# Mish and the attention copies ahead of the weight decodings in slots 4 to 15 of a three-stage kernel

## The chip, the cores and the metric

One core of a Trainium2 chip runs the whole program in one launch. The metric is device time in microseconds (us), the median of several runs. The matrix engine is called PE, the vector engine DVE, the scalar engine ACT, GpSimd POOL, and SP issues most of the DMAs.

## The reference

Three stages follow each other. Attention without softmax (4 batches, 8 heads, 576 tokens, 64 per head) gives 2304 tokens of 512 values; two feed-forward stages follow, each 512 to 2048 to 512, the first with Mish, the second with a leaky ReLU whose slope is learned.

```python
kv  = einsum('bhsd,bhse->bhde', k, v)
out = einsum('bhsd,bhde->bhse', q, kv)
x   = out / sqrt(mean(out*out, -1) + 1e-6) * g_norm      # then 2304 x 512
h   = x @ w_in1;  g = h * tanh(softplus(h));  x = g @ w_out1
h   = x @ w_in2;  g = max(h,0) + alpha*min(h,0);  out = g @ w_out2
```

The weights come as 64-bit floats and are read as pairs of 32-bit words.

## The kernel before, in words

A product of fp32 matrices is made of three fp32r products of a high and a low half (`three`, lines 135 to 137): high by high, high by low, low by high. So every operand has to be split first, on ACT (the cast that makes the high half) and DVE (the subtraction that makes the low half).

The first feed-forward stage goes over five blocks of tokens (512, 256, 512, 512, 512). A block has 16 slots, one for each 128 columns of the hidden layer; slots are numbered through. In slot s PE makes

- `mm1(s)`, 12 matmuls, the hidden values h of slot s;
- pieces of the attention of the next block (the hooks): `t_pe` transposes q (L257), `kv_pe` makes k times v (L232), `o_pe` multiplies q by it (L289);
- `mm2(s - 4)`, 12 matmuls, which adds the part of slot s - 4 to four output accumulators.

Between `mm1` and `mm2` lie `mish(s)` on ACT (L547, from h to the tile n) and `g_split(s)` (the cast to gh on ACT, L540, and the subtraction to gl on DVE, L541). `mish(s - 1)` stands in slot s (`front`), `g_split(s - 2)` at the end of slot s (`back`). Two buffers each limit this: `mish(s)` writes the n that `g_split(s - 2)` has read, and `mm1(s)` writes the bank of h that `mish(s - 2)` has read (`bank("h", ...)`, two banks).

In slots 4 to 15, the first block, the weights of this stage are decoded on the way, about two tiles of 128x512 words in each slot (three in slot 7): `w_begin` scales the high words on ACT (`w_scale`, L432), joins the words by three operations on DVE (`w_bits`, L438, L439, L442), and then finishes the tile that was begun before it: its cast on ACT (`w_high`, L477) and its subtraction on DVE (`w_low`, L481). L438 reads the low words; L439 reads the scaled high words, so it waits for L432. The decoding of a tile of `w_in1` stands in the list `mid` of a slot, that of a tile of `w_out1` in `last`.

The attention of the next block is spread over `hook`, two entries in a slot (2s and 2s + 1). After `kv_pe` come two small copies from PSUM (`kv_ev`, L244, on ACT), which `o_pe` needs; after `o_pe` a square and a copy (L296, L297). In slot 10 the hook `rsqrt_ev` part 0 loads another activation table, computes two functions (L341, L342, L345), and loads Mish's table again (L346).

From slot 4 to slot 25 the order of all engines is the order in which the code is written (`manual_schedule`); from slot 26 on only PE's is, and a scheduler orders the rest. Each engine works through its own list strictly from the front: an instruction that waits holds up all behind it on that engine.

Of the kernel before, what the change touches and what calls it, by code (L numbers as in the profile page):

```python
# [33 lines left out]
EARLY = 4  # L34
# [23 lines left out]
def attn_moe_moe2(  # L58
# [37 lines left out]
    NJ = DFF // P  # L96
# [36 lines left out]
    def three(ps, lhs, rhs, start, stop, **kw):  # L133
        (lh, ll), (rh, rl) = lhs, rhs
        nc.tensor.matmul(ps, lh, rh, start=start, stop=False, **kw)  # L135
        nc.tensor.matmul(ps, lh, rl, start=False, stop=False, **kw)  # L136
        nc.tensor.matmul(ps, ll, rh, start=False, stop=stop, **kw)  # L137
# [74 lines left out]
    def bank(tag, nm):  # L212
        if tag == "at":
            turn[0] += 1
            tag = f"at{turn[0] % 2}"
        pool = ps_h if tag == "h" else ps_a if tag[:2] == "at" else ps_acc
        return pool.tile([P, 512], F32, tag=tag, name=nm)
# [287 lines left out]
    def at_slot(kk):  # L505
        i = kk // NJ
        return i, kk % NJ, BLOCKS[i]

    def mm1(kk, chunks=range(4)):
        i, j, T = at_slot(kk)  # L510
        if chunks[0] == 0:
            hps[kk] = bank({2: "at1", 3: "acc3"}.get(kk, "h"), "h")
        ps = hps[kk]
        wh, wl = w1[0, j]
        for c in chunks:
            cs = slice(c * P, (c + 1) * P)
            three(ps[:, :T], (wh[:, cs], wl[:, cs]), (xh[i, c], xl[i, c]), c == 0, c == NP - 1)

    def mm2(kk):
        i, j, T = at_slot(kk)  # L520
        gh, gl = gt.pop(kk)
        wh, wl = w2[0, j]
        if j == 0:
            acc[i] = [None] * NP
        for m in range(NP):
            ms = slice(m * P, (m + 1) * P)
            if j == 0:
                acc[i][m] = bank(f"acc{m}", "acc")
            three(acc[i][m][:, :T], (wh[:, ms], wl[:, ms]), (gh, gl), j == 0, j == NJ - 1)
        if j == NJ - 1:  # L530
            evac(i)
# [4 lines left out]
    def g_split(kk):  # L536
        T = at_slot(kk)[2]
        g = gs.pop(kk)
        gh, gl = m_tile("gh", T, F32R), m_tile("gl", T, F32R)
        nc.scalar.copy(out=gh, in_=g)  # L540
        nc.vector.tensor_tensor(out=gl, in0=g, in1=f32(gh), op=ALU.subtract)  # L541
        gt[kk] = gh, gl

    def mish(kk):
        T = at_slot(kk)[2]
        g = m_tile("n", T)
        nc.scalar.activation(out=g, in_=hps.pop(kk)[:, :T], func=AF.Mish)  # L547
        gs[kk] = g
# [3 lines left out]
    def evac(i):  # L552
        a = acc.pop(i)
        T = BLOCKS[i]
        if not x2d:
            x2d.append(dp.tile([P, NP, NT], F32, name="x2d"))
        for c in range(0, NP, 2):
            xs = stage("xs", F32, 2 * T)
            nc.scalar.copy(out=xs[:, :T], in_=a[c][:, :T])
            nc.vector.tensor_copy(out=xs[:, T:], in_=a[c + 1][:, :T])  # L560
            nc.sync.dma_start(
                out=x2d[0][:, c : c + 2, starts[i] : starts[i] + T], in_=xs.rearrange("p (c t) -> p c t", c=2)
            )
# [363 lines left out]
    loads, early, after, late, hook, mid, fin, last = ({} for _ in range(8))  # L927
# [4 lines left out]
    def run(d, s):  # L932
        for f, a in d.pop(s, []):
            f(*a)
# [71 lines left out]
    def front(s):  # L1006
        if EARLY < s <= NS:
            mish(s - 1)

    def back(s):  # L1010
        if LAG <= s < NS + LAG:
            mm2(s - LAG)
        if s - 2 < NS:
            g_split(s - 2)

    def slot(s):
        for d in (early, loads) if s == EARLY else (loads, early):
            run(d, s)
        mm1(s)

        run(mid, s)
        run(hook, 2 * s)
        run(after, s)
        run(late, s)
        front(s)
        run(last, s)
        run(fin, s)
        back(s)
        run(hook, 2 * s + 1)
# [6 lines left out]
    def quarter(n):  # L1036

        s = NS + n
        u, step = divmod(n, 4)
        run(early, s)  # L1040
        run(late, s)

        def before(step):
            front(s)
            run(mid, s)
            back(s)
            if step == 3 or u:
                chunk(u if step == 3 else u - 1, LATER[step])

        if long(u):  # L1050
            long_unit(u, step)
            if step == 1:
                before(0)
                before(1)
            elif step == 3:
                before(2)
                prelu1(u, "12", tmp["x"], tmp["x"])
                before(3)
        elif u < NPASS * NU:
            unit(u, step, lambda: before(step))  # L1060
        else:
            before(step)
        run(fin, s)
        run(last, s)
# [32 lines left out]
    with tc.manual_schedule():  # L1097
# [36 lines left out]
        for s in range(EARLY, MANUAL):  # L1134
            slot(s)
    with tc.manual_schedule(engines={mybir.EngineType.PE}):
        for s in range(MANUAL, NS):
            slot(s)
        for n in range(4 * NPASS * NU + 3):
            quarter(n)  # L1140
# [30 lines left out]
```

## Time and profile before

| what | value |
|---|---|
| median of 3 runs | 837.09 us (836.38 to 839.85) |
| the profiled execution: its own time | 837.51 us |
| the profiled execution: its span | 835.7 us |
| granted TensorE clock, mean | 0.999 of full speed |
| ACT busy | 318.9 us (38%) |
| POOL busy | 42.9 us (5%) |
| matmuls | 4446 |

Times of the trace are counted from the start of the span. The page's busy share tells how long an engine had something in work. A matmul overlaps the next, so its duration is longer than the step to the next one; whether PE was held up is read from the steps between starts and from the idle time. The first block's slots 4 to 15 lie between about 36 and 112 us.

### The profile page before, as it was taken

Reading aid. Unit: us, or ns where it says so; the run is one execution under the profiler, and the core shown is the slowest. Engines: PE = TensorE matmul, PEld = TensorE weight load, DVE = VectorE, ACT = ScalarE, POOL = GpSimd, SP = SyncE. Lnnn points to the kernel's source line nnn. Section 1 sums busy time; section 2 is a strip of 40 time slices with the busy share of each in tenths; the row PEclk is TensorE's granted clock in tenths of the full one; section 3 lists DMA queues with packets and bytes.
Section 4 is the critical chain, followed back from the end, with each engine's and each line's share of the span. In section 5 each row is a group of like instructions: output and inputs, shape, how many; then the busy total and the mean of one; then the engine's idle time right before and its main releaser. Section 6 shows DMA issues by size and latency. Waiting matters only on the chain.

```text
span 835.7 us, 11757 instructions
## 1 busy us (share of the span) xinstructions
PE 826.6 (99%) x4446; PEld 710.4 (85%) x4446; DVE 534.5 (64%) x1001; ACT 318.9 (38%) x630; POOL 42.9 (5%) x52
## 2 busy tenths in 40 slices
PE   8999999999999999999999999999999999999998
PEld 6777789998878887888788889889999999899896
DVE  6998873552275334543978777889654668754644
ACT  5768555344433442433555322234111124211112
POOL 0000000000302121030400000000000000000000
PEclk9999999999999999999999999999999999999999
DMA  8974447244131413039995614232411332311212
GB/s 294 286 208 145 137 94 164 53 79 131 49 99 44 145 45 114 1 138 370 341 368 180 189 51 151 89 126 64 126 38 39 82 107 74 116 38 40 74 38 76
DMA packets 84377, 104.59 MB, mean 125 GB/s; under 512 B 34785, under 2 KB 57569, under 8 KB 84321
## 3 DMA queue, kind: packets, MB, share of 16 engines
q1 hardware_dynamic: 84176, 103.71, 40.0%
q8 instruction: 35, 0.57, 0.3%
q14 instruction: 22, 0.17, 0.1%
q10 hardware_dynamic: 144, 0.13, 0.0%
HBM read 79.70 MB, written 24.12 MB: 124 GB/s over the span
## 4 chain that ended last, share of the span: by engine, by line
PE 89%; DVE 5%; DMA 2%; ACT 2%; issue 0%; SPq 0%; DVEq 0%; ACTq 0%
PE acc L136 15%; PE acc L137 15%; PE acc L135 15%; PE pp L137 7%; PE pp L135 7%; PE pp L136 7%; PE h L135 7%; PE h L136 7%; PE h L137 7%; DMA ws<-in_moe_w_out_dram 1%; PE kvps L232 1%; DVE wf L439 1%; DVE wf L442 1%; DMA v<-in_v_dram 1%; PE ops L289 0%
## 5 line engine op out<-in xcount | busy, mean ns | idle before, releaser
L135 PE MATMUL acc<-gh,w 128*128 128x512 f32 (+1 forms) x320 | 119.3, 373 | 0.0
L136 PE MATMUL acc<-gl,w 128*128 128x512 f32 (+1 forms) x320 | 117.9, 368 | 0.0
L137 PE MATMUL acc<-gh,w 128*128 128x512 f32 (+1 forms) x320 | 117.9, 368 | 0.0
L541 DVE TENSOR_TENSOR gl<-n,gh 128x512 fp32r<-128x512 f32 (+1 forms) x80 | 51.7, 648 | 95.1 <-ACT gh L540 94.9
L135 PE MATMUL h<-x,w 128*128 128x512 f32 (+1 forms) x240 | 90.6, 378 | 1.2 <-ACT n L547 1.1
L137 PE MATMUL h<-x,w 128*128 128x512 f32 (+1 forms) x240 | 88.6, 369 | 0.0
L136 PE MATMUL h<-x,w 128*128 128x512 f32 (+1 forms) x240 | 88.4, 368 | 0.0
L540 ACT CAST gh<-n 128x512 fp32r<-128x512 f32 (+1 forms) x80 | 46.3, 578 | 106.8 <-PE acc L137 106.2
L137 PE MATMUL acc<-w,g 128*128 128x512 f32 x216 | 85.2, 394 | 0.0
L808 ACT CAST g<-ty 128x384 fp32r<-128x384 f32 x48 | 24.7, 514 | 138.1 <-DVE ty L806 138.0
L135 PEld LDWEIGHTS acc<-gh,w 128*128 128x128 f32 x320 | 60.3, 189 | 10.3 <-issue 0.4
L137 PEld LDWEIGHTS acc<-gh,w 128*128 128x128 f32 x320 | 60.3, 188 | 10.2
L136 PEld LDWEIGHTS acc<-gl,w 128*128 128x128 f32 x320 | 60.4, 189 | 9.8
L547 ACT ACTIVATE n<-h 128x512 f32<-128x512 f32 (+1 forms) x80 | 44.5, 556 | 34.4 <-DVE gl L541 34.3
L136 PE MATMUL acc<-w,xb 128*128 128x512 f32 x144 | 56.6, 393 | 0.0
L136 PE MATMUL acc<-w,g 128*128 128x512 f32 x144 | 56.6, 393 | 0.0
L135 PEld LDWEIGHTS h<-x,w 128*128 128x128 f32 x240 | 45.2, 188 | 13.0 <-ACT n L547 3.1
L135 PE MATMUL acc<-w,xb 128*128 128x512 f32 x144 | 56.0, 389 | 0.0
L135 PE MATMUL acc<-w,g 128*128 128x512 f32 x144 | 56.0, 389 | 0.0
L137 PEld LDWEIGHTS h<-x,w 128*128 128x128 f32 x240 | 45.2, 188 | 8.1 <-DVE w L481 0.4
L136 PEld LDWEIGHTS h<-x,w 128*128 128x128 f32 x240 | 45.3, 189 | 7.2
L137 PEld LDWEIGHTS acc<-w,g 128*128 128x128 f32 x216 | 40.5, 188 | 8.6
(230 smaller groups left out, 1706.6 us busy)
## 6 DMA issues: line engine op xcount, KB each, us to landing
xb<-wd SPq DMA_DIRECT2D x72, 256.0 KB, 2.7
ws<-in_moe_w_out_dram SPq DMA_DIRECT2D x32, 512.0 KB, 4.2
xw<-in_moe_w_in_dram SPq DMA_DIRECT2D x12, 512.0 KB, 5.6
r<-in_moe_w_in_dram SPq DMA_DIRECT2D x12, 512.0 KB, 4.2
wd<-r SPq DMA_DIRECT2D x12, 512.0 KB, 2.6
w<-wd SPq DMA_DIRECT2D x12, 512.0 KB, 6.6
k<-in_k_dram SPq DMA_DIRECT2D x16, 288.0 KB, 3.5
v<-in_v_dram SPq DMA_DIRECT2D x16, 288.0 KB, 4.5
```

Of the source, the lines that this page charges most:

```text
L135: nc.tensor.matmul(ps, lh, rh, start=start, stop=False, **kw)
L136: nc.tensor.matmul(ps, lh, rl, start=False, stop=False, **kw)
L137: nc.tensor.matmul(ps, ll, rh, start=False, stop=stop, **kw)
L232: nc.tensor.matmul(ps[hs, hs], kt[:, h, j, :], vt[:, h, j, :], start=(j == 0), stop=(j == KVJ - 1))
L439: nc.vector.scalar_tensor_tensor(out=si, in0=high, scalar=-0x80000000, in1=si, op0=ALU.bitwise_and, op1=ALU.bitwise_or)
L442: nc.vector.scalar_tensor_tensor(out=si, in0=high, scalar=3, in1=si, op0=ALU.logical_shift_left, op1=ALU.bitwise_or)
L540: nc.scalar.copy(out=gh, in_=g)
L541: nc.vector.tensor_tensor(out=gl, in0=g, in1=f32(gh), op=ALU.subtract)
L547: nc.scalar.activation(out=g, in_=hps.pop(kk)[:, :T], func=AF.Mish)
L808: nc.scalar.copy(out=h, in_=out)
```

## The change

In slot 4 the hook 9 (`kv_pe`, `kv_ev`) moves in front of `g_split(2)`, and both in front of the decoding in `last`. In slots 5 to 15 `front(s)`, which is `mish(s - 1)`, moves from behind `mid`, the even hook, `after` and `late` to a place right behind `mm1(s)`, ahead of `mid`. Nothing is added or removed.

```diff
-    def back(s):
+    def back(s, between=lambda: None):
         if LAG <= s < NS + LAG:
             mm2(s - LAG)
+        between()
         if s - 2 < NS:
             g_split(s - 2)
...
         mm1(s)
+        if s == EARLY:
+
+            run(mid, s)
+            run(hook, 2 * s)
+            back(s, lambda: run(hook, 2 * s + 1))
+            for d in (late, last, fin):
+                run(d, s)
+            return
+
+        sooner = EARLY < s < NJ
+        if sooner:
+            front(s)
 
         run(mid, s)
         run(hook, 2 * s)
         run(after, s)
         run(late, s)
-        front(s)
+        if not sooner:
+            front(s)
```

PE's list and SP's list of DMAs keep their order; ACT's list changes in slots 4 to 15, and DVE's in slot 4 alone.

On ACT in slot 4, from the copy of transposed q (L270) on, before (`keep` holds k times v, `gh` is slot 2's, w16 is a tile of `w_in1`, `ws` the raw words of the next tile):

```order
L270 COPY qT_545<-tps_542 128x256
L432 ACTIVATE ws_515<-ws_515 128x512
L477 CAST w16_552<-wf_535 128x512
L540 CAST gh_571<-n_485 128x512
L244 COPY keep_87<-kvps_575 64x64 x2
```

and with the change:

```order
L270 COPY qT_545<-tps_542 128x256
L244 COPY keep_87<-kvps_563 64x64 x2
L540 CAST gh_578<-n_485 128x512
L432 ACTIVATE ws_515<-ws_515 128x512
L477 CAST w16_587<-wf_535 128x512
```

The two copies and the cast of gh moved ahead of the scaling and the cast of the decoding.

On ACT at the border of slots 5 and 6, before (`xw` holds the raw words of the tile decoded in `mid`, n is Mish's result of slot 5):

```order
L540 CAST gh_651<-n_492 128x512
L270 COPY qT_658<-tps_655 128x256
L432 ACTIVATE xw_95<-xw_95 128x512
L477 CAST w23_681<-wf_632 128x512
L244 COPY keep_87<-kvps_684 64x64 x2
L547 ACTIVATE n_708<-h_602 128x512
L432 ACTIVATE ws_590<-ws_590 128x512
```

and with the change:

```order
L540 CAST gh_651<-n_492 128x512
L270 COPY qT_658<-tps_655 128x256
L547 ACTIVATE n_676<-h_602 128x512
L432 ACTIVATE xw_95<-xw_95 128x512
L477 CAST w23_683<-wf_632 128x512
L244 COPY keep_87<-kvps_686 64x64 x2
L432 ACTIVATE ws_590<-ws_590 128x512
```

Mish (L547) moved ahead of the scaling of the first tile of slot 6, of a cast and of the copies of k times v.

On ACT in slot 10, where the activation table is changed, before:

```order
L432 ACTIVATE xw_95<-xw_95 128x512
L477 CAST w27_975<-wf_924 128x512
L341 ACT_TABLE_LOAD
L342 ACTIVATE qT_658<-msps_978,epsb_94 128x256
L345 ACTIVATE qT_775<-qT_658 128x256
L346 ACT_TABLE_LOAD
L547 ACTIVATE n_987<-h_885 128x512
L432 ACTIVATE ws_883<-ws_883 128x512
```

and with the change:

```order
L547 ACTIVATE n_970<-h_885 128x512
L432 ACTIVATE xw_95<-xw_95 128x512
L477 CAST w27_977<-wf_924 128x512
L341 ACT_TABLE_LOAD
L342 ACTIVATE qT_658<-msps_980,epsb_94 128x256
L345 ACTIVATE qT_777<-qT_658 128x256
L346 ACT_TABLE_LOAD
L432 ACTIVATE ws_883<-ws_883 128x512
```

Mish moved from behind the second table load to the front of the slot; the second tile's scaling stays behind that load.

## Rows read from the trace of the kernel before

**Rows 1.** The page's busy times, and one stretch of the windows view (start:end us, length, busy us of PE, PEld, DVE, ACT, POOL, clock, DMA share, GB/s).

```profile
PE 826.6 (99%) x4446; PEld 710.4 (85%) x4446; DVE 534.5 (64%) x1001; ACT 318.9 (38%) x630; POOL 42.9 (5%) x52
50.00:60.00 10.00, 10.00 (x69) 8.12 (x67) 9.52 (x16) 7.45 (x17) 0.00 (x0) 1.00 0.89 242
```

**Rows 2.** Timeline of ACT, slot 4 (start us, duration us, engine, line, operation, out<-in).

```profile
43.97 0.68 ACT L432 ACTIVATE ws<-ws 128x512 f32<-128x512 f32 x1
...
46.08 0.42 ACT L244 COPY keep<-kvps 64x64 f32<-64x64 f32 x2
```

**Rows 3.** Timeline of PE, slot 5 (in brackets the idle time before, and its releaser).

```profile
41.92 0.92 PE L232 MATMUL kvps<-v,k 96*64 96x64 f32 x24
...
45.62 0.33 PE L289 MATMUL ops<-qT,keep 128*128 128x64 f32 x2
46.56 0.59 PE L289 MATMUL ops<-qT,keep 128*128 128x192 f32 x2 [0.60 <-ACT keep L244]
```

**Rows 4.** Timeline of DVE, the end of slot 5 and the beginning of slot 6.

```profile
53.76 0.68 DVE L541 TENSOR_TENSOR gl<-n,gh 128x512 fp32r<-128x512 f32 x1
54.36 0.42 DVE L438 TENSOR_SCALAR wf<-xw 128x512 int32<-128x512 int32 x1
54.89 0.69 DVE L439 SCALAR_TENSOR_TENSOR wf<-xw,wf 128x512 int32<-128x512 int32 x1
```

**Rows 5.** Timeline of ACT in slot 6: the scaling for that L439, then Mish.

```profile
52.00 0.68 ACT L432 ACTIVATE xw<-xw 128x512 f32<-128x512 f32 x1
...
54.48 0.60 ACT L547 ACTIVATE n<-h 128x512 f32<-128x512 f32 x1 [0.26 <-DVE gl L541]
54.97 0.69 ACT L432 ACTIVATE ws<-ws 128x512 f32<-128x512 f32 x1
```

**Rows 6.** Timeline of ACT in slot 10, around the two table loads.

```profile
78.49 0.62 ACT L477 CAST w<-wf 128x512 fp32r<-128x512 f32 x1
79.12 1.28 ACT L341 ACT_TABLE_LOAD   x1
80.76 0.47 ACT L342 ACTIVATE qT<-msps,epsb 128x256 f32<-128x256 f32 x1 [0.35 <-PE msps L331]
81.26 0.42 ACT L345 ACTIVATE qT<-qT 128x256 f32<-128x256 f32 x1
81.70 1.28 ACT L346 ACT_TABLE_LOAD   x1
82.99 0.60 ACT L547 ACTIVATE n<-h 128x512 f32<-128x512 f32 x1
```

**Rows 7.** Timeline of DVE: gl at the end of slots 9 to 12, and L439 waiting or first behind.

```profile
78.97 0.68 DVE L541 TENSOR_TENSOR gl<-n,gh 128x512 fp32r<-128x512 f32 x1
...
84.17 0.69 DVE L439 SCALAR_TENSOR_TENSOR wf<-ws,wf 128x512 int32<-128x512 int32 x1 [1.60 <-ACT ws L432]
...
86.11 0.68 DVE L541 TENSOR_TENSOR gl<-n,gh 128x512 fp32r<-128x512 f32 x1
...
88.03 0.69 DVE L439 SCALAR_TENSOR_TENSOR wf<-ws,wf 128x512 int32<-128x512 int32 x1
...
92.83 0.68 DVE L541 TENSOR_TENSOR gl<-n,gh 128x512 fp32r<-128x512 f32 x1
...
94.05 0.69 DVE L439 SCALAR_TENSOR_TENSOR wf<-ws,wf 128x512 int32<-128x512 int32 x1 [0.20 <-ACT ws L432]
...
98.58 0.69 DVE L541 TENSOR_TENSOR gl<-n,gh 128x512 fp32r<-128x512 f32 x1
```

**Rows 8.** Timeline of PE: the first matmul of `mm1(13)` and of `mm1(14)`.

```profile
95.08 0.50 PE L135 MATMUL h<-x,w 128*128 128x512 f32 x1 [0.24 <-ACT n L547]
...
100.96 0.40 PE L135 MATMUL h<-x,w 128*128 128x512 f32 x1
```

**Rows 9.** Timeline in slot 16: DVE's low half of w_out1's tile 12, PE's first use of it.

```profile
112.91 0.68 DVE L481 TENSOR_TENSOR w<-wf,w 128x512 fp32r<-128x512 f32 x1
...
114.17 0.39 PE L137 MATMUL acc<-gh,w 128*128 128x512 f32 x1
```

## The prediction

> **What bounds the kernel now.** I read the page's busy times first, then PE's idle times and step lengths slot by slot, and then the timelines of ACT and DVE beside them. PE is busy for 826.6 of 835.7 us [rows 1], so no reordering of the other engines can give back much; what it can do is to take away single waits of PE, or to make new ones. In the first block DVE is the engine that can make them: between 50 and 60 us it is busy for 9.52 of 10 us, and PE for all 10 [rows 1]. DVE has hardly any slack there, and ACT, busy for 7.45, has some.
>
> PE is held up visibly at two places in slots 4 to 15. In slot 5 the second part of `o_pe` starts 0.94 us after the first, 0.60 of it idle, until the copies of k times v end [rows 3]. These copies run at 46.08 although their input was ready at 42.84 (41.92 + 0.92): the scaling that started at 43.97, and more, stood ahead of them [rows 2, 3]. In slot 13 `mm1` has to wait for Mish, 0.24 us idle [rows 8]. The reader should keep both in mind as all that the change can win here: taken between idle time and lost step, 0.8 + 0.4 = 1.2 us.
>
> **What decides Mish's start.** Mish of slot s - 1 overwrites the n that gl of slot s - 3 is made from, and that gl is the last thing in DVE's list of slot s - 1. In slot 6 one sees it: gl runs from 53.76 to 54.44 [rows 4], and Mish starts at 54.48, after ACT had idled for 0.26 us waiting for just this [rows 5]. So even at its old, late place Mish waited for DVE. At its new place it waits for the same end of gl, but now with the scaling of the next tile, its cast, the copies of k times v and all else of the slot queued behind it on ACT.
>
> **Slot 4.** The copies move ahead of a scaling, a cast and the cast of gh, to where the scaling starts now, 43.97 [rows 2]. They take 0.42, so they are done 1.2 us before `o_pe` starts at 45.62 [rows 3]. PE's wait goes: 0.60 (the idle time) to 0.94 (the whole step), taken as 0.8. On DVE gl of slot 2 only changes places with the four operations of one decoding, with no work added; I cost that at nothing. The cover is that the low half of the tile needed next gets finished some 0.5 us later, one place of 0.6 down the list, still ahead of its use by PE; without that lead `mm1(6)` would wait 0.6 at most.
>
> **Slots 6 to 9, the term that matters.** DVE begins these slots with L438 and L439 of the tile in `mid`. Before, the scaling that L439 needs was done long ago (52.00 for an L439 at 54.89), and L439 started 0.45 us after gl's end (54.89 - 54.44) [rows 4, 5]. Now the order after gl's end is: 0.04 to Mish's start (54.48 - 54.44), 0.49 from Mish to the next instruction (54.97 - 54.48), 0.69 for the scaling, and for the handover to L439 another 0.04: 1.26 [rows 4, 5]. DVE therefore loses 1.26 - 0.45 = 0.81 us in every slot that begins this way with no wait before: slots 6, 7, 8 and 9, so 4 x 0.81 = 3.2 us. Slot 5 is spared, since a whole decoding stands between gl of slot 2 and the tile of slot 5's `mid`.
>
> **Slot 10, with the table loads.** Here DVE waited already: gl ended at 79.65 and the L439 of the second tile started at 84.17, 4.52 later, after 1.60 idle for ACT's scaling [rows 7]. ACT had reached the table loads at 79.12, before gl's end, because Mish stood behind them [rows 6]. Now everything follows gl's end: 0.04, Mish 0.49, scaling 0.58 (0.69 less the overlap of 0.11 that Mish shows), cast 0.63, table 1.29, 0.50, 0.44, table 1.29, scaling 0.69, handover 0.04: 5.99 us [rows 5, 6]. That is 5.99 - 4.52 = 1.5 us more. The 0.35 that ACT waited for PE [rows 6] falls away, as PE's sums are ready long before; no term of the sum holds it.
>
> For a table I use 1.29, since the rows show 1.28 for the load and the next instruction 0.01 behind the second one's end (81.70 + 1.28, then 82.99) [rows 6]. A rule of the Trainium skill speaks against the change more strongly: ScalarE: Activation LUTs, section What ACT_TABLE_LOAD costs, gives 1.28 us for the load and another 1.38 for a drain behind it. By that rule the two loads would add 2.8 us to this slot and to the sum; the second load here shows no such drain.
>
> **Slots 11 and 12.** In slot 11 two operations of the attention lie between gl (ended 86.79) and L439 (88.03): 1.24 already, so the new 1.26 costs nothing. In slot 12 L439 followed gl's end by 0.54, a late load included (94.05 - 93.51) [rows 7]; now 1.26, so 0.7 more. From slot 13 on no tile is decoded in `mid`, and the scaling behind Mish is needed later.
>
> **The sum.** DVE's delay at the end of slot 12 is 3.2 + 1.5 + 0 + 0.7 = 5.4 us: gl that ended at 99.27 [rows 7] ends at 104.67. On the way PE waits again and again, for copies of k times v that now stand behind Mish, and for Mish itself; those waits are not added, for the last one on the same chain contains them, and slot 4's 0.8 with them. Mish of slot 12 starts 0.04 later and lasts 0.60, and `mm1(14)` follows at about 105.35 (another handover) where it started at 100.96 [rows 8]: 4.4 us. A first matmul after a wait lasts 0.50 where one without lasts 0.40 [rows 8], so 0.1 more. In slot 16 PE first used the low half of tile 12 at 114.17, 0.58 after DVE had it (113.59) [rows 9]; with DVE 5.4 late and PE 4.5, PE waits about 0.3 again (0 if DVE has regained some by then). Sum: 4.4 + 0.1 + 0.3 = **4.8 us slower**, with bounds 4.2 (without slot 16, and 0.07 less in each of slots 6 to 9) and 5.5 (one more 0.7 as in slot 12). Behind slot 16 the order is the same on every engine and PE sets the pace, so the delay stays. The profiled execution would go from 837.51 to 842.3; it stands 0.42 above the median, so against the median of 837.09 I forecast 841.9.
>
> **The rivals.**
>
> *The waits go and nothing comes in their place.* If gl were done before ACT comes to the front of a slot, Mish would start at once, and the change would win the 1.2 us of slots 5 and 13: 835.9. The point at which it decides is whether DVE ends a slot's list ahead of ACT. Against it speak the 0.26 us that ACT idled for gl and DVE's 9.52 of 10 [rows 1, 5]. Chance 0.04. This is the other side in sign, though its size, 0.14%, is within what a measurement can tell.
>
> *DVE's lead takes up the delay.* Decoded tiles are needed a slot or more later, so part of DVE's delay may never reach PE, if the slots' own slack gives back what each Mish costs. Then little is left, between -1 and +2 us, about 837.6. For it: most tiles are ready some us ahead. Against it: Mish feeds the bank that PE needs next, and in slot 13 PE waited for it already, with no slack [rows 8]. Chance 0.10.
>
> *The switch of tables costs more on the path.* Behind the first load comes a wait of 0.35 for PE that could hide a part of its price, and behind the second none [rows 6]. If a switch on the path cost the length of a second load, that would be 2 x 1.28 = 2.6 us more: 844.5. The 0.01 behind the second load speaks against it. Chance 0.04. It is the mechanism of the rule of the Trainium skill, ScalarE: Activation LUTs, told above.
>
> **How the numbers follow.** The forecast has 0.82. About 0.5%, 4.2 us, is what a measurement of this kernel can tell from no change, so the border lies at 841.3, just under the forecast. Of the forecast's 0.82 I put 0.62 above that border and 0.20 below it. Slower: 0.62 and the tables' 0.04, 0.66. Same: 0.20, the lead's 0.10 and most of the first rival's 0.04: 0.33. Faster by that much would need 832.9, which only some other effect could bring: 0.01. The forecast's own bounds are 841.3 and 842.6; three runs of one kernel spread over 3.5 us (836.38 to 839.85), so each end is moved out by half of that: 839.5 to 844.3. That leaves out the first two rivals and, just, the third.
>
> **What would show it.** Right: L439 idle for about 0.8 us for ACT's scaling (L432) in slots 6 to 9, and for about 2 in slot 10; Mish starting 0.04 after gl in slots 6 to 13; PE idle for Mish before `mm1(12)`, `mm1(13)` and `mm1(14)`, and for the copies before `o_pe` in slots 8 and 9; no wait in slot 5 any more; the same step lengths after 125 us, shifted by 4.8. Wrong: Mish waiting for PE and not for gl, DVE without idle time in slots 6 to 9, or a delay at slot 16 below 3 us. A gap between Mish and the scaling, or behind a table load, would show a size wrong.

## The result and the profile after

The changed kernel takes 842.60 us (median of 5 runs, 841.89 to 843.59) where the kernel before takes 837.20 (now 5 runs): the ratio is 1.0059, 95% interval 1.0048 to 1.0071, so 4.0 to 5.9 us slower. 841.9 was forecast. The profiled execution took 842.37 us, 4.86 more than that of before, with a span of 840.5.

The page's busy times, and its group of PE's high-by-high matmuls into h (at the end the idle time before them, 1.2 us in the kernel before, and its releaser):

```profile
PE 828.2 (99%) x4446; PEld 711.1 (85%) x4446; DVE 534.1 (64%) x1001; ACT 318.1 (38%) x630; POOL 42.9 (5%) x52
L135 PE MATMUL h<-x,w 128*128 128x512 f32 (+1 forms) x240 | 90.7, 378 | 3.6 <-ACT n L547 3.6
```

Every engine ran the same instructions as before; DVE and ACT were busy as long within 0.8 us, PE 1.6 us longer [rows 1]. What is new is waiting. PE's waits between 30 and 126 us (us in total, times, longest), before 0.6 for the copies `keep` and 0.2 for Mish, once each, are now:

```profile
PE h L135 <- ACT n L547: 2.6, 3, 1.3
PE ops L289 <- ACT keep L244: 1.8, 3, 0.8
```

The timeline of DVE shows where these come from: gl at the end of slots 5, 9, 10, 11 and 12, and every L439 that waits in slots 6 to 12 (idle time and releaser in brackets).

```profile
54.09 0.68 DVE L541 TENSOR_TENSOR gl<-n,gh 128x512 fp32r<-128x512 f32 x1
...
55.98 0.69 DVE L439 SCALAR_TENSOR_TENSOR wf<-xw,wf 128x512 int32<-128x512 int32 x1 [0.87 <-ACT xw L432]
...
62.39 0.69 DVE L439 SCALAR_TENSOR_TENSOR wf<-xw,wf 128x512 int32<-128x512 int32 x1 [0.87 <-ACT xw L432]
...
71.43 0.69 DVE L439 SCALAR_TENSOR_TENSOR wf<-xw,wf 128x512 int32<-128x512 int32 x1 [0.90 <-ACT xw L432]
...
77.85 0.69 DVE L439 SCALAR_TENSOR_TENSOR wf<-xw,wf 128x512 int32<-128x512 int32 x1 [0.87 <-ACT xw L432]
...
82.37 0.68 DVE L541 TENSOR_TENSOR gl<-n,gh 128x512 fp32r<-128x512 f32 x1
...
84.26 0.69 DVE L439 SCALAR_TENSOR_TENSOR wf<-xw,wf 128x512 int32<-128x512 int32 x1 [0.87 <-ACT xw L432]
...
88.97 0.69 DVE L439 SCALAR_TENSOR_TENSOR wf<-ws,wf 128x512 int32<-128x512 int32 x1 [2.23 <-ACT ws L432]
...
90.91 0.69 DVE L541 TENSOR_TENSOR gl<-n,gh 128x512 fp32r<-128x512 f32 x1
...
97.62 0.68 DVE L541 TENSOR_TENSOR gl<-n,gh 128x512 fp32r<-128x512 f32 x1
...
99.52 0.69 DVE L439 SCALAR_TENSOR_TENSOR wf<-ws,wf 128x512 int32<-128x512 int32 x1 [0.88 <-ACT ws L432]
...
104.05 0.68 DVE L541 TENSOR_TENSOR gl<-n,gh 128x512 fp32r<-128x512 f32 x1
```

In each of slots 6 to 10 and 12, DVE now waits 0.87 to 0.90 us for the scaling of the tile that it begins with; in slot 6 L439 ran straight on before [rows 4]; in slot 10 it waits 2.23 more. The timeline of ACT says why. In slot 6 Mish waits for gl's end, and the scaling for Mish (54.09 + 0.68 = 54.77, Mish 54.80, scaling 55.30 to 55.95, L439 at 55.98):

```profile
54.80 0.60 ACT L547 ACTIVATE n<-h 128x512 f32<-128x512 f32 x1 [2.38 <-DVE gl L541]
55.30 0.65 ACT L432 ACTIVATE xw<-xw 128x512 f32<-128x512 f32 x1
55.84 0.61 ACT L477 CAST w<-wf 128x512 fp32r<-128x512 f32 x1
56.35 0.42 ACT L244 COPY keep<-kvps 64x64 f32<-64x64 f32 x2
```

ACT idles 2.38 us in front of Mish, with all its work of the slot queued behind it. In slot 10 the two table loads come behind Mish too, and the scaling of the second tile behind them:

```profile
83.08 0.60 ACT L547 ACTIVATE n<-h 128x512 f32<-128x512 f32 x1 [1.97 <-DVE gl L541]
83.58 0.65 ACT L432 ACTIVATE xw<-xw 128x512 f32<-128x512 f32 x1
84.12 0.61 ACT L477 CAST w<-wf 128x512 fp32r<-128x512 f32 x1
84.75 1.28 ACT L341 ACT_TABLE_LOAD   x1
86.05 0.48 ACT L342 ACTIVATE qT<-msps,epsb 128x256 f32<-128x256 f32 x1
86.56 0.42 ACT L345 ACTIVATE qT<-qT 128x256 f32<-128x256 f32 x1
86.99 1.28 ACT L346 ACT_TABLE_LOAD   x1
88.29 0.65 ACT L432 ACTIVATE ws<-ws 128x512 f32<-128x512 f32 x1
```

On PE the delay arrives at the copies in slots 6, 8 and 9 (the 1.8 us above; slot 6 was not in the prediction's list), at the first matmuls of `mm1(12)`, `mm1(13)` and `mm1(14)`, and once more in slot 16:

```profile
92.28 0.50 PE L135 MATMUL h<-x,w 128*128 128x512 f32 x1 [1.27 <-ACT n L547]
...
98.99 0.50 PE L135 MATMUL h<-x,w 128*128 128x512 f32 x1 [0.98 <-ACT n L547]
...
105.41 0.50 PE L135 MATMUL h<-x,w 128*128 128x512 f32 x1 [0.39 <-ACT n L547]
...
118.43 0.40 PE L136 MATMUL acc<-gl,w 128*128 128x512 f32 x1
118.83 0.50 PE L137 MATMUL acc<-gh,w 128*128 128x512 f32 x1
```

The steps of 0.40 and then 0.34 around 118.83 (before, 0.24 and 0.22) are the wait for the low half of tile 12. The wait of slot 5 [rows 3] is gone: `o_pe` runs in one piece from 45.92.

### The profile page after: what moved, and what is told of

It is laid out like the page before. It is cut to its first block, busy times and chain, and to the rows that moved or that the text cites. A ratio compares the mean times of both kernels' runs of the same rounds, so it can differ in the third digit from the quotient of the medians.

```text
span 840.5 us, 11758 instructions
## 1 busy us (share of the span) xinstructions
PE 828.2 (99%) x4446; PEld 711.1 (85%) x4446; DVE 534.1 (64%) x1001; ACT 318.1 (38%) x630; POOL 42.9 (5%) x52
## 4 chain that ended last, share of the span: by engine, by line
PE 83%; DVE 8%; DMA 4%; ACT 3%; issue 1%; SPq 0%; DVEq 0%; ACTq 0%
PE acc L137 14%; PE acc L136 14%; PE acc L135 14%; PE pp L137 7%; PE pp L135 7%; PE pp L136 7%; PE h L135 6%; PE h L136 6%; PE h L137 6%; DMA r<-in_moe_w_in_dram 2%; DVE wf L439 2%; DMA q<-in_q_dram 1%; DVE w L481 1%; DVE wf L442 1%; DVE gl L541 1%
## 5 line engine op out<-in xcount | busy, mean ns | idle before, releaser
L547 ACT ACTIVATE n<-h 128x512 f32<-128x512 f32 (+1 forms) x80 | 44.5, 556 | 53.6 <-DVE gl L541 53.3
```

## The experiments

Theory A is the prediction's: DVE loses its time because the scaling that it needs stands behind Mish, and Mish behind DVE's own gl. Theory B puts the loss on PE's direct waits for work that stands behind Mish on ACT, the copies of k times v above all. Theory C blames slot 4's new order.

The ratio is to runs of the kernel before made alongside (medians 837.20, 837.97 and 837.76 us in the three sets). Beside it the table gives the stretch of slots 5 to 16, read from PE's timeline in one profile of each kernel: from the first matmul of `mm1(5)`, up to which PE has the same work in all of them, to that of `mm1(17)`. Before it is 73.67 us (42.77 to 116.44). How far a stretch repeats is told at the end; differences under 0.2 us should not be read.

| kernel | ratio to before (95%) | stretch, us | against before |
|---|---|---|---|
| the change | 1.0059 (1.0048 to 1.0071) | 78.20 | +4.53 |
| slot 4 alone | 1.0003 (0.9994 to 1.0011) | 73.88 | +0.21 |
| Mish alone | 1.0060 (1.0045 to 1.0075) | 78.99 | +5.32 |
| the change, scaling ahead of Mish | 1.0007 (0.9997 to 1.0016) | 73.81 | +0.14 |
| the change, third n | 0.9977 (0.9968 to 0.9986) | 72.36 | -1.31 |
| the change, but for slot 10 | 1.0031 (1.0020 to 1.0041) | 76.44 | +2.77 |
| scaling ahead of Mish, not in slot 10 | 0.9989 (0.9980 to 0.9998) | 72.76 | -0.91 |
| slot 4, and Mish in slot 10 alone | 1.0019 (1.0010 to 1.0028) | 75.35 | +1.68 |
| before, third n | 0.9998 (0.9989 to 1.0006) | 73.56 | -0.11 |

**Slot 4 alone.**

```diff
-        sooner = EARLY < s < NJ
+        sooner = False
```

> The change's slot 4 alone; Mish stays at its old place in slots 5 to 15. Theory A (all of the loss comes from DVE waiting for a scaling that is queued behind Mish, which waits for gl): no loss is left, within 0.5 us of before, about 837.2. The wait of 0.60 us before o_pe in slot 5 goes, but gl of slot 2 now stands ahead of four operations of a decoding on DVE, so the cast behind them and with it Mish of slot 4, which still stands behind that cast, come some 0.5 us later and mm1(6) waits for that Mish; net 0.0 (-0.2 to +0.3). Theory B (the waits for the copies of k times v are the loss): the copies in slot 4 are early, so a gain of 0.8, 836.4. Theory C (slot 4's new order starts the loss): +1 us or more.

Measured: no loss and no gain. The wait at `o_pe` is gone and another has come, in the timelines of ACT and PE of this kernel:

```profile
48.56 0.62 ACT L477 CAST w<-wf 128x512 fp32r<-128x512 f32 x1 [1.38 <-DVE wf L442]
49.21 0.39 ACT L296 ACTIVATE qT<-ops 128x256 f32<-128x256 f32 x1
49.49 0.37 ACT L297 COPY o<-ops 128x256 f32<-128x256 f32 x1
49.74 0.61 ACT L547 ACTIVATE n<-h 128x512 f32<-128x512 f32 x1
```

```profile
50.41 0.50 PE L135 MATMUL h<-x,w 128*128 128x512 f32 x1 [0.67 <-ACT n L547]
```

gl moved ahead of a decoding on DVE; the cast behind that decoding came later, and Mish, at its old place behind the cast, made `mm1(6)` wait for 0.67 us. Theory C falls, and B's gain of 0.8 did not come. Slot 4's edit pays only if Mish doesn't stand behind that cast.

**Mish alone.**

```diff
-        if s == EARLY:
+        if False:
```

> Mish at the front of slots 5 to 15, slot 4 in its old order. Theory A: slot 5 now begins on DVE right behind gl of slot 2 as slots 6 to 9 do, so it pays the same 0.8 us: five slots and not four, L439 of slot 5 idle for 0.8 to 0.9, and about 5.5 us slower than before, 842.7 (842.0 to 843.5), some 0.8 above the change itself. Theory B: the old wait of 0.8 in slot 5 comes back and the rest stays, 5.6 as well, but L439 of slot 5 isn't idle. Theory C: little is left, under 2 us.

Measured: 0.8 us more in the stretch than the change itself (78.99 - 78.20); in the whole time the two can't be told apart. In the timeline of DVE slot 5 now pays as well:

```profile
48.85 0.69 DVE L541 TENSOR_TENSOR gl<-n,gh 128x512 fp32r<-128x512 f32 x1
49.45 0.42 DVE L438 TENSOR_SCALAR wf<-xw 128x512 int32<-128x512 int32 x1
50.76 0.69 DVE L439 SCALAR_TENSOR_TENSOR wf<-xw,wf 128x512 int32<-128x512 int32 x1 [0.89 <-ACT xw L432]
```

This is A's point against B: L439 idles in slot 5 as soon as gl of slot 2 stands right in front of it. The 0.8 by itself fits both theories, as the old wait for the copies in slot 5 is back too.

**The scaling ahead of Mish.** One instruction of the change is moved:

```diff
         if sooner:
+            for n, (f, w) in enumerate(mid.get(s, [])):
+                if f is w_begin:
+                    w_scale(*w)
+                    mid[s][n] = w_scaled, w
             front(s)
...
+    def w_scaled(*w):
+        w_bits(*w)
+        w_end()
+        begun.append(w)
```

> The change, with one instruction moved: in slots 5 to 15 the scaling of the mid tile (L432) stands ahead of Mish, and its cast, the copies of k times v and all else stay behind Mish. Theory A: DVE no longer waits at the beginning of slots 6 to 9 (3.1 us) and 12 (0.7); only slot 10 stays, where the second scaling stands behind Mish and two table loads: some 0.5 to 1.0 us, against 0.5 to 0.9 won in slots 5 and 13. About 837.6, +0.4 (-0.3 to +1.2). L439 idle under 0.2 us in slots 6 to 9 and about 1.6 to 2.2 in slot 10. Theory B: copies and casts still stand behind Mish, so PE's waits for them stay: +3 us or more, 840.5.

Measured: the loss is gone (+0.07%, +0.14 us in the stretch). In slot 6, in the timelines of DVE and ACT, gl's end and Mish's wait stay, and L439 runs straight on (L546 and L552 are gl and Mish in this kernel):

```profile
54.84 0.68 DVE L546 TENSOR_TENSOR gl<-n,gh 128x512 fp32r<-128x512 f32 x1
55.44 0.42 DVE L438 TENSOR_SCALAR wf<-xw 128x512 int32<-128x512 int32 x1
55.97 0.69 DVE L439 SCALAR_TENSOR_TENSOR wf<-xw,wf 128x512 int32<-128x512 int32 x1
```

```profile
53.08 0.70 ACT L432 ACTIVATE xw<-xw 128x512 f32<-128x512 f32 x1
55.56 0.60 ACT L552 ACTIVATE n<-h 128x512 f32<-128x512 f32 x1 [1.78 <-DVE gl L546]
56.05 0.61 ACT L477 CAST w<-wf 128x512 fp32r<-128x512 f32 x1
56.56 0.42 ACT L244 COPY keep<-kvps 64x64 f32<-64x64 f32 x2
```

The casts and copies still stand behind Mish, and PE no longer waits for them. But with the scaling out of the way the copies also start 1.00 us after Mish's start (56.56 - 55.56), where it was 1.55 in the change (56.35 - 54.80), so this run by itself doesn't tell B from A, and no run moved the copies alone. What tells them apart is what DVE waits for in the change between 42 and 105 us (us in total, times, longest):

```profile
DVE wf L439 <- ACT xw L432: 4.4, 5, 0.9
DVE wf L439 <- ACT ws L432: 3.1, 2, 2.2
```

DVE waits there for scalings alone and not for PE, so it was not PE's waits for the copies that made it late; and the Mish that `mm1(14)` waits for starts 0.03 us after DVE's gl. So theory B falls.

What is left isn't quite where it was expected. L439 waits in slot 10 (2.47 us), but PE's one wait for Mish, 1.19 us at `mm1(13)`, is behind a transfer, since the scaling of slot 12 stands ahead of Mish here and its words landed late:

```profile
95.06 0.67 ACT L432 ACTIVATE ws<-ws 128x512 f32<-128x512 f32 x1 [2.57 <-DMA ws<-in_moe_w_in_dram]
95.64 0.58 ACT L552 ACTIVATE n<-h 128x512 f32<-128x512 f32 x1
```

The transfer of these words was issued at 91.38, 0.07 us after the first decoding of slot 11 on DVE ended (91.31). Counted from `mm1(5)` that decoding ended 0.81 us later than in the kernel before, behind the second L439 of slot 10, which was 0.80 later. So slot 10's wait on DVE reaches PE here through a buffer that came free late.

**A third buffer for n.**

```diff
-        g = m_tile("n", T)
+        third = EARLY <= kk < NJ - 1 and kk % 3 == 1
+        g = wp.tile([P, 2 * DM], F32, tag=f"w2{NJ - 1}", name="n3")[:, :T] if third else m_tile("n", T)
```

> The change, with a third buffer for n in the first block (a piece of a weight's room that is free then), so that Mish of slot s - 1 waits for the gl of slot s - 4 and not of slot s - 3. Theory A: Mish starts at once at the front of a slot, nothing queues behind it, and what is left is the gain: the waits in slots 5, 11 and 13 go, about -0.9 us, 836.3 (-1.3 to -0.3). No idle time of L439 in slots 6 to 9. A theory that Mish's own time in front of the scaling costs DVE its slot's beginning, whether it waits or not: 0.5 us in each of four or five slots stays, +2 to +2.5. Theory B: the copies stand behind Mish as before, +1 or more.

Measured: faster than the kernel before and than the change, 0.9977, and in the stretch -1.31 us, at the far end of what was expected. Mish runs at once in slot 6, 1.8 us before gl is made, in the timelines of ACT and DVE (L548 is Mish in this kernel):

```profile
51.92 0.60 ACT L548 ACTIVATE n<-h 128x512 f32<-128x512 f32 x1
52.41 0.69 ACT L432 ACTIVATE xw<-xw 128x512 f32<-128x512 f32 x1
```

```profile
53.68 0.68 DVE L541 TENSOR_TENSOR gl<-n,gh 128x512 fp32r<-128x512 f32 x1
54.28 0.42 DVE L438 TENSOR_SCALAR wf<-xw 128x512 int32<-128x512 int32 x1
54.81 0.69 DVE L439 SCALAR_TENSOR_TENSOR wf<-xw,wf 128x512 int32<-128x512 int32 x1
```

Mish stands in front of the scaling here exactly as in the change. So it isn't Mish's own 0.5 us that DVE lost, but Mish's wait for gl. PE has one wait left between 30 and 126 us:

```profile
PE kvps L232 <- ACT qT L270: 0.2, 1, 0.2
```

**The change, but for slot 10.**

```diff
-        sooner = EARLY < s < NJ
+        sooner = EARLY < s < NJ and s != 10
```

> The change, but slot 10 (the one with the two table loads) keeps Mish at its old place. Theory A, by its own terms: slots 6 to 9 have delayed DVE by 3.1 us, and slot 10's further 1.4 falls away; Mish of slot 9 now comes behind both table loads, after gl, so mm1(11) waits for it, and slot 12 then finds 0.7 that PE has already lost. About +2.9 against before, 840.8 (840.0 to 841.5). If the table loads were what makes the change slow, within 1 us of before.

Measured: +2.77 us in the stretch, +0.31% in all. Mish's move in slot 10, the slot with the table loads, isn't the whole loss; it is 1.8 of it (4.53 - 2.77).

**Scaling ahead of Mish, and slot 10 as before.** Both edits above together.

> The scaling of the mid tile ahead of Mish in slots 5 to 15, and Mish at its old place in slot 10. Theory A: with the scaling ahead and the table loads not behind Mish, none of the terms of the loss is left, and the waits of slots 5 and 13 are gone in part: -0.7 us against before, 837.3 (-1.2 to 0), L439 idle under 2 us in slots 6 to 12 together. Theory B (the casts and copies behind Mish cost PE): +1 us or more. The step from mm1(12) to mm1(13), 1.2 us longer than without a wait in the run with the scaling ahead in all slots, is back at 5.5 to 5.9.

Measured: -0.91 us in the stretch, 0.9989. From `mm1(12)` to `mm1(13)` it takes 5.44 us. Without a third buffer, too, the change's idea gives a small gain once the scaling isn't held up and slot 10 is left as it was.

**Slot 10 alone** (`sooner = s == 10`).

> The change's slot 4, and Mish at the front of slot 10 alone. Theory A: DVE isn't late when slot 10 begins, gl to L439 of the second tile takes 5.9 us as it did in the change's own profile and not 4.5, and that 1.4 us reaches PE through Mish at mm1(12) and mm1(13): +1.4 against before, 839.4 (838.6 to 840.0). If single delays of this size are taken up by DVE's lead: within 0.5 us.

Measured: +1.68 us in the stretch, 1.0019; against slot 4 alone, from which it differs in slot 10 only, +1.47 (75.35 - 73.88). PE loses it in two parts: `mm1(11)` to `mm1(12)` takes 6.44 us, before 5.59, and `mm1(12)` to `mm1(13)` 6.71, before 5.85. Only the first comes straight from DVE. In slot 12 Mish stands at its old place, behind a scaling whose words landed late, as in the run with the scaling ahead:

```profile
94.98 0.69 ACT L432 ACTIVATE ws<-ws 128x512 f32<-128x512 f32 x1 [2.93 <-DMA ws<-in_moe_w_in_dram]
```

**The third buffer with the old order.**

> The kernel before with the third buffer for n alone, all engines in the old order. If the gain with the third buffer came from the buffer and not from Mish's place: -0.9 us or better, about 836.5. Theory A: at its old place Mish stands behind the scaling, the casts and the copies anyway, and the waits of slots 5 and 13 are for what stands in front of it, so the buffer alone changes nothing: within 0.3 us of before.

Measured: nothing (0.9998). The buffer pays only with Mish at the front (and slot 4's edit, which was not tried with the buffer by itself); Mish at the front pays only with the buffer, or with the scaling ahead and slot 10 left out.

## Why the prediction was right, point by point

The terms can be read off as growth of gl's delay from slot to slot, rows of before [rows 4, 7] against those above; each gl is the one at the end of the slot named. gl of slot 5 starts 0.33 later (54.09 against 53.76); 0.30 of this was there at `mm1(5)` (43.07 against 42.77), ahead of anything that the change touches, and belongs to no term.

| term | forecast, us | measured, us |
|---|---|---|
| slots 6 to 9 (gl of slot 9: 82.37 - 78.97 - 0.33) | 3.2 | 3.07 |
| slot 10 (90.91 - 86.11 - 3.40) | 1.5 | 1.40 |
| slot 11 (97.62 - 92.83 - 4.80) | 0 | 0.0 |
| slot 12 (104.05 - 98.58 - 4.79) | 0.7 | 0.68 |
| DVE's delay, sum | 5.4 | 5.14 |
| `mm1(14)` (105.41 - 100.96 - 0.30), and what its wait adds up to `mm1(16)` | 4.4 + 0.1 | 4.15 + 0.04 |
| slot 16 (4.51 - 4.17, `mm1(16)` to `mm1(17)`) | 0.3 | 0.34 |
| sum | 4.8 | 4.53 |

- **Mish's start.** It came 0.03 to 0.04 us after gl's end in slots 6 to 13, where 0.04 was forecast. Taking the wait away with a third buffer turned the loss of 4.5 into a gain of 1.3: this step is shown.
- **Slots 6 to 9.** 0.77 us each against 0.81, because the scaling behind Mish lasts 0.65 (0.68 in slot 8) and not 0.69. Moving the scaling removed the term: shown.
- **Slot 10.** The sum of 5.99 from gl's end was 5.92 (88.97 - 83.05). The table loads took 1.28 and the next instruction followed 0.02 later, both times. So the rival of the dearer switch falls. The Trainium skill (ScalarE: Activation LUTs, What ACT_TABLE_LOAD costs) adds 1.38 us of drain to each load; here the next instruction started after 0.02, so that drain did not show.
- **The first matmul after a wait.** At `mm1(14)` the step to the next matmul was 0.34 us where it was 0.24, as forecast. But from `mm1(14)` to `mm1(16)` it took 11.35 us (105.41 to 116.76), before 11.31 (100.96 to 112.27): the later steps gave all but 0.04 of it back. This term was too large; why the later steps were shorter, the runs don't show.
- **Slot 4.** Here the prediction was incomplete. In the change PE's 0.8 did go (from `mm1(5)` to `mm1(6)` 6.29 us, before 7.12). But the swap of gl and a decoding on DVE, costed at nothing, delays the cast behind it, and alone it gives the whole gain back through Mish. In the sum this made no difference, as Mish no longer stands behind that cast there; the prediction had not seen that cast, so it was right here by luck. That slot 5 is spared was right, and worth 0.8 us, as Mish alone shows.
- **The rivals.** PE's waits did not go without replacement; the point named, whether gl is done before ACT comes to the front of a slot, decided it, with ACT idle for 1.7 to 2.9 us in front of Mish. DVE's lead didn't take up the delay: Mish at the front of slot 10 alone, with 1.4 us of delay on DVE (gl's end to the second L439 5.96 us, from 79.64 to 85.60, against 4.52), cost PE 1.5 against slot 4 alone.
- **The total.** Of the profiled execution's 4.86 us, 4.53 are the change's and 0.30 lie ahead of it. The medians differ by 5.4. How much of the 0.9 between that and the stretch is scatter, the runs don't settle; the interval, 4.0 to 5.9, takes in both numbers. That the median of 842.60 lies only 0.7 from the forecast is in part luck: the terms came out 0.3 too large, and the whole time came out above them.

## What to carry to other kernels

In front of an instruction that is moved ahead on an in-order engine, look for what it will wait for at its new place, and then for everything that will stand behind it. If it waits for the last work of a busy engine, and that engine's next work needs something queued behind it, each turn costs the busy engine a round trip (here 0.77 us a slot), although nobody does more work. Then move what the busy engine needs ahead as well, or break the wait with one more buffer; either change alone can be worth nothing, as the buffer was here, or lose, as the move did.

## What the runs showed that was not expected

The time at which `mm1(5)` starts varies from 42.67 to 43.83 us over the profiles of these ten kernels, though what PE does up to there is the same in all of them. It is settled within the first 12 us: PE's second group of matmuls for k times v starts between 10.08 and 11.23 us, and `mm1(5)` follows 32.56 to 32.67 us after it in all ten. PE's waits for the first tiles of v, up to 1.45 us in eight of the ten, fall in this time, but their length alone doesn't tell the start: the kernel before waits for 1.18 us and is among the earliest. That is 1.2 us of scatter from the start of the program, as much as the whole gain that was to be had.

A stretch between two matmuls leaves this out, and the intervals of the whole times reach 0.7 to 1.3 us to either side. But each stretch is from one profile. Slot 7, in which PE shows no wait, took 6.78 to 6.82 us in all ten kernels; slot 12 took 5.85 in the kernel before and 5.70 in the same with a third n, where what Mish stands behind waits for a transfer. So 0.2 us between two stretches is about the least that can be told.
